# Transfers of 49 rows padded to 56 rows, a third buffer for stage D's constants, and longer planned landings

## The chip, the cores and the metric

The kernel runs on one core of one Trainium2 chip. The metric is the device time of one execution in microseconds (us). The core works with TensorE (PE: matrix products, its weight loads appear as PEld), VectorE (DVE), ScalarE (ACT), GpSimd (POOL), SyncE (SP, which here only issues transfers) and 16 DMA engines.

## What is computed

The reference chains two blocks on x of shape (8, 3136, 256), in float32:

```python
def _attn_ref(x, w_r, w_i, b_r, b_i):
    X = np.fft.rfft(x, axis=1)
    Yr = X.real @ w_r - X.imag @ w_i + b_r
    Yi = X.real @ w_i + X.imag @ w_r + b_i
    Y = shrink(Yr, 0.01) + 1j * shrink(Yi, 0.01)      # soft threshold
    return np.fft.irfft(Y, n=x.shape[1], axis=1)

def _moe_ref(x, U, V, w_ch1, w_ch2):
    xt = x.transpose(0, 2, 1)
    h = xt @ U @ V                                    # along the sequence, rank 32
    u = x + h.transpose(0, 2, 1)
    ch = np.maximum(u @ w_ch1, 0.0) @ w_ch2           # 256 -> 1024 -> 256
    return u + ch
```

(`shrink` stands for the reference's sign and maximum.)

## The kernel before, in words

The 3136 positions of one batch entry are split as 49 x 64, so that each Fourier transform becomes two steps of small matrix products. The work of one batch b goes through stages, and arrays in HBM lie between them:

- Stage A (`a_load` L702, `a_mm` L713): eight tiles `xt` (the first six of batch 1: `xa`) are loaded from x, each with two transfers of 49 rows of 4 KB, one into partitions 0 to 48 and one into 64 to 112. The 49-point transform with the matrix `fq` goes into PSUM (`psa`), is copied back over the tile, and four transfers of 49 rows of 2 KB put it into the HBM array `gd`. Batch 0 takes another way (`xx`, `t0t`).
- Stages B and C (`load_t`, `b_unit` L899, `mix_unit`, `c_unit` L982): 12 or 13 rounds per batch. `t` is loaded from `gd` and `fb` from the constants, 64-point transform (`psb`), channel mix (`psq`, `pst`), soft threshold (`rl`, `ys`, `yh`, `yl`), transform back (`psc`, copied to `zs`), store into the HBM array `zd`. A round begins on ACT with copies of `psb` to `xsh` and to the single buffer `ts`.
- Stage D (`z_load` L1071, `dt_load` L1078, `d_unit` L1086): eight tiles `zt` are loaded from `zd`, again with two transfers of 49 rows of 4 KB each, and six pieces `dt` of D's constants (128 rows, held in the HBM array `dud`, two buffers). The products `psd` give 49 positions, copied by ACT to `xq`, and 32 columns for U, summed by DVE into `pa`.
- P (`p_spread` L1156, `p_unit` L1164): DVE adds the parts of `pa` into `pr`, PE transposes it (`psp`), ACT and DVE make `pt` of it, the input of the product with V.
- Windows: six of 512 positions x 256 channels per batch (and one last one for the rest, 49 in all). `u_prep` adds the V product (`psv`) and splits into high and low parts (`oa`, `ob`, `oc`, `od`), `l1_chunks` is the first product of the channel block (`psx`, `psy`, `psz`), with `s`, `v`, `rh`, `rl` on ACT and DVE behind it, `l2_chunks` the second (`pso`). `out_unit` (L1731) transposes the result on DVE into the single buffer `os` (two instructions) and stores it with four transfers to `out_dram`.

While the windows of batch b run, stages B, C and D of batch b+1 and stage A of batch b+2 are put between them. The tiles `xt` and `zt` share five buffers (tag `xz`).

No engine's order is written out by hand. The kernel records all its operations, and a planner (`_Program.order`, L259) lays them out: a list scheduler that gives each operation a cost and a delay until its result is there (`cost`, L193), grants buffers, and serves on each engine the operation with the earliest due time. It goes forwards and backwards in time 12 times, takes the due times of the best pass, and issues everything in the order of its planned starts (`trace`, all from L537, so every row of the profile has that line, and groups are told apart by tiles). For a transfer the plan takes 64,000 elements per us and a landing 2.2 us behind that (L202, L504), and it lets a transfer start at most 16 us before it is due. SP issues all transfers but three, in one order, and each engine works its own list strictly in order.

Of the kernel before, what the change touches and what calls it, by code (L numbers as in the profile page):

```python
# [13 lines left out]
F32 = mybir.dt.float32  # L14
# [10 lines left out]
NB = 8  # L25
N1, N2 = 49, 64
NP = 98
NI = 32
D = 256
R = 32  # L30
# [10 lines left out]

STEPS_W = 8
K1 = 49
C81 = K1 + R

UNITS_D = [(0, 6), (6, 6), (12, 4), (16, 6), (22, 6), (28, 4)]
# [117 lines left out]
class _Program:  # L164
# [28 lines left out]
    def cost(self, op, out, ins):  # L193
        n = out.ids.size // out.shape[0] if isinstance(out, _View) else 1
        sb = not any(v.buf.space == "psum" for v in ins)
        op.move, op.port, op.fill, op.mode = 0.0, False, 0, 0
        if op.name == "dma_start":

            some = out if isinstance(out, _View) else ins[0]
            op.move = some.ids.size / 64000  # L200
            op.cost = 0.35 if op.eng == "act" else 0.6
            op.lag = 2.2 + op.move  # L202
        elif op.eng == "pe":
            if "tile_position" in op.kw:

                op.cost = (0.001668 * n + 0.005) / (4 if op.kw["lhsT"].shape[0] <= 64 else 2)
                op.mode = 2
            elif op.name == "matmul" and op.kw["lhsT"].dtype == F32:
                op.cost = 2 * max(0.111, 0.00084 * n)
                op.mode = 1  # L210
            else:
                op.cost = max(0.1118, 0.000422 * n)
            op.lag = 0.25
        elif op.eng == "act":
            op.cost = 0.062 + 0.000844 * n + (0.036 if sb else 0) + (0.098 if "bias" in op.kw else 0)
            op.lag = 0.2
        elif op.eng == "dve":

            op.port = sb and op.name != "transpose"
            slow = op.name == "transpose" and not sb  # L220
            op.cost = 0.07 + (0.00053 if op.name == "tensor_scalar" else 0.00158 if slow else 0.00104) * n
            op.lag = 0.185
        elif op.eng == "pool":
            op.port = op.name == "tensor_tensor"
            op.cost = 0.1 + (0.00223 if op.port else 0.0007) * n
            op.lag = 0.19
# [160 lines left out]
    def forward(self, units, size, tags, gap, late):  # L387

        engines = ("pe", "act", "dve", "pool", "sp")
        free = dict.fromkeys(engines, 0.0)  # L390
# [51 lines left out]
        while done < len(units):  # L442
            best = None
            for e in engines:
                now = max(free[e], moved - 2.0, landed[-8]) if e == "sp" else free[e]
                while future[e] and future[e][0][0] <= now:
                    _, l, k = _heapq.heappop(future[e])
                    _heapq.heappush(ready[e][units[k][0].mode if e == "pe" else units[k][0].port], (l, k))

                may = []  # L450
                if e == "pe":
                    for m in range(3):
                        if m == 2 and mode == 2 and not ready[e][2]:

                            soon = [f for f in future[e] if units[f[2]][0].mode == 2 and f[0] < now + TILED_WAIT]
                            if soon:
                                t, l, k = min(soon)
                                may = [(t, l, k, 4)]
                        elif ready[e][m]:
                            l, k = ready[e][m][0]  # L460
                            if m == 1 and mode == 1:
                                l -= STICK
                            elif m == 2:
                                l += -TILED_STAY if mode == 2 else TILED_IN
                            may.append((now, l, k, m))
                else:
                    if ready[e][0]:
                        may.append((now, *ready[e][0][0], 0))
                    if ready[e][1]:
                        may.append((max(now, port), *ready[e][1][0], 1))  # L470
                if not may and future[e]:
                    t, l, k = future[e][0]
                    may.append((max(t, port) if units[k][0].port else t, l, k, 3))
                if may and (best is None or min(may)[:2] < best[:2]):
                    best = *min(may), e
            if best is None:
                break
            t, l, k, kind, e = best
            if kind == 4:
                future[e].remove(next(f for f in future[e] if f[2] == k))  # L480
                _heapq.heapify(future[e])
            else:
                _heapq.heappop(future[e] if kind == 3 else ready[e][kind])
            u = units[k][0]
            if e == "pe":
                if t > free[e]:
                    self.idle.append((free[e], t - free[e], u))

                b = u.out.buf
                gap_, each = t - max(free[e], b.granted) - 0.2, 0.222  # L490
                if done_pe == 0:

                    gap_, each = gap_ - 0.6, 0.47
                done_pe += 1
                fill[k] = max(0, int(gap_ / each)) if b.first[0] is u and t < FILL else 0
            free[e] = t + sum(op.cost for op in units[k])
            if e == "pe":
                free[e] += SWITCH[mode][u.mode]
                mode = u.mode
            elif u.port:  # L500
                port = free[e]
            if u.move:
                moved = max(moved, t) + u.move
                u.lag = moved + 2.2 - free[e]  # L504
                landed.append(moved + 2.2)
            starts[k] = t
            done += 1
            for op in units[k]:
                op.start = t + op.at
                for s in op.succs:  # L510
                    if s.unit != k:
                        release(s.unit, t + gap(op, s) - s.at)
                bs = {}
                for v in list(op.args) + list(op.kw.values()):
                    if isinstance(v, _View) and v.buf.space != "dram":
                        bs[id(v.buf)] = v.buf
                for b in bs.values():
                    b.left -= 1
                    b.end = max(b.end, op.start + op.cost + op.lag)
                    if b.left == 0:  # L520
                        _heapq.heappush(slots[b.key], (b.end, k, b.slot, b))
                        grant(b.key)
# [18 lines left out]
def fft_mix_moe_kernel(  # L541
# [116 lines left out]
    bias = const.tile([128, 2, D], F32, name="bias")  # L658
    lam = const.tile([128, 1], F32, name="lam")

    gd = [dram.tile([N1, N2, D], F32, name=f"gd{k}") for k in range(2)]
    zd = [dram.tile([N1, N2, D], F32, name=f"zd{k}") for k in range(2)]
    dud = dram.tile([128, NI * C81], F32, name="dud")
    vd = dram.tile([2, R, 96 * NI], F32, name="vd")
    rd = dram.tile([128, 2, NB, 64], F32, name="rd")
# [31 lines left out]
            h, d = divmod(16 * k, 128)  # L697
            dve.transpose(out=t0[h][:, :, d : d + 16].rearrange("p k d -> p d k"), in_=ps.rearrange("p i d -> p d i"))

    xj = x.rearrange("b (n j i) d -> b j n i d", j=2, i=NI)  # L700

    def a_load(b, c):  # L702
        if b == 1 and c < 6:
            if c % 3 == 0:
                ahead_x[c // 3] = qp.tile([128, 12, D], F32, tag="xq", name=f"xa_{c}", bufs=3)
            xt = ahead_x[c // 3][:, 4 * (c % 3) : 4 * (c % 3) + 4]
        else:
            xt = fp.tile([128, 4, D], F32, tag="xz", name=f"xt_{b}_{c}", bufs=5)
        loads = [dma.dma_start(xt[64 * j : 64 * j + K1], xj[b, j, :, 4 * c : 4 * c + 4]) for j in range(2)]
        a_state[b, c] = xt  # L710
        return loads

    def a_mm(b, c, loads=()):  # L713
# [19 lines left out]
        for j in range(2):  # L733
            o = xt[:, 2 * j : 2 * j + 2]
            p = ps[j].rearrange("p (i d) -> p i d", i=2)
            if j:
                dve.tensor_copy(o, p)
            else:
                acopy(o, p)
            for e in range(2):  # L740
                i = 4 * c + 2 * e
                dma.dma_start(gv[j, :, i : i + 2], o[64 * e : 64 * e + K1])

    def a_half(b, half, loads):
        for c in range(4):
# [325 lines left out]
    def z_load(b, c):  # L1071
# [1 line left out]
        zt = fp.tile([128, 4, D], F32, tag="xz", name=f"zt_{b}_{c}", bufs=5)  # L1073
        zv = zd[b % 2].rearrange("k (j c i) d -> c j k i d", j=2, i=4)
        s_state[b, "z", c] = zt
        return [dma.dma_start(zt[64 * j : 64 * j + K1], zv[c, j]) for j in range(2)]

    def dt_load(b, t):  # L1078
        n0, n = UNITS_D[t]
        dt_ = mp.tile([128, 6 * C81], F32, tag="dt", name=f"dt_{b}_{t}", bufs=2)  # L1080
        dma.dma_start(dt_[:, 0 : n * C81], dud[:, n0 * C81 : (n0 + n) * C81])
        s_state[b, "d", t] = dt_

# [1 line left out]

    def d_unit(b, t, du, loads=()):  # L1086
        if t == 0:
            p_state[b] = qp.tile([128, 2, 3, R], F32, tag="pa", name=f"pa_{b}", bufs=2)
        n0, n = UNITS_D[t]
        hf = n0 // NH  # L1090
        if n0 % NH == 0:
# [62 lines left out]
        return us  # L1154

    def p_spread(b):  # L1156
        pr = qp.tile([128, 2, 4, R], F32, tag="pr", name=f"pr_{b}", bufs=1)
        pa = p_state[b]
        dve.tensor_tensor(out=pa[:, :, 0], in0=pa[:, :, 0], in1=pa[:, :, 1], op=ALU.add)
        a, c = [pa[:, :, k].unsqueeze(2).broadcast_to([128, 2, 4, R]) for k in (0, 2)]  # L1160
# [618 lines left out]
    for st in u0:  # L1779
        st()  # L1780
    setup_w()
    side = []

    def spread(units, lo, hi):
# [151 lines left out]
```

## Time and profile before

| What | us |
|---|---|
| Time before, median of 3 runs | 1676.95 |
| lowest and highest of them | 1668.06, 1677.43 |
| the profiled execution | 1668.87 |
| its span, first to last instruction | 1667.1 |

The profile is of one execution, 8.1 us below the median; 1.8 us of it lie outside the span. PE is busy in 96% of the span, DVE in 78%, ACT in 56%. A busy PE is not a PE at its peak: the ends of matmuls are modelled, and at the lower of TensorE's two clock levels (1.2 instead of 2.4 GHz) the same work takes twice as long and is counted as busy all the same. The column PEclk is the granted clock as a share of the full one. The share of the DMA engines is a mean over all 16.

### The profile page before, as it was taken

The page shows a single profiled execution, that of the slowest core. Times are in us where ns is not written, and L with a number is a line of the kernel's source. Part 1 is how long each engine was busy: PE and PEld are TensorE (multiplying, and loading weights), DVE is VectorE, ACT ScalarE, POOL GpSimd, SP SyncE. Part 2 cuts the span into 40 slices and gives each one's busy share as a digit, 9 for nine tenths or more (in the row PEclk, how much of TensorE's full clock was granted, in tenths as well). Part 3 has the DMA queues.
Part 4 walks back from the last instruction along what each step waited for, and adds up shares of the span by engine and source line. Part 5 has one row for each costly group of instructions (what it writes and reads, how often), then busy time and mean ns, then how long its engine had stood idle before and what let it go on. Part 6 is the DMA issues. An engine that isn't in the chain of part 4 may idle for free.

```text
span 1667.1 us, 37824 instructions
## 1 busy us (share of the span) xinstructions
PE 1607.3 (96%) x14546; PEld 1441.1 (86%) x14546; DVE 1299.8 (78%) x2478; ACT 932.2 (56%) x1982; POOL 449.6 (27%) x406
## 2 busy tenths in 40 slices
PE   8998999999989999899999999999999999999998
PEld 6967898899878889799888988989977999989997
DVE  7576888588956899678975889769985699957775
ACT  4764566556545665456654566555654566545453
POOL 1310333133311333123321133313331133412221
PEclk9989999999999999999998999999998999999999
DMA  9754343515552354522745244532555224530232
GB/s 232 218 178 159 93 145 96 159 44 131 164 152 83 118 162 116 151 59 66 175 147 156 79 143 128 145 89 68 148 146 166 66 67 98 111 113 13 53 75 47
DMA packets 229775, 198.30 MB, mean 119 GB/s; under 512 B 129594, under 2 KB 197728, under 8 KB 229596
## 3 DMA queue, kind: packets, MB, share of 16 engines
q1 hardware_dynamic: 226958, 195.02, 42.9%
q8 instruction: 115, 1.88, 0.5%
q10 hardware_dynamic: 2638, 0.86, 0.3%
q14 instruction: 64, 0.52, 0.1%
HBM read 118.92 MB, written 76.90 MB: 117 GB/s over the span
## 4 chain that ended last, share of the span: by engine, by line
PE 68%; DMA 14%; DVE 12%; issue 2%; ACT 2%; SPq 2%; DVEq 0%; ACTq 0%
PE pso L537 23%; PE psy L537 14%; PE psx L537 6%; PE psq L537 5%; DMA out_dram<-os 4%; PE psb L537 4%; PE psd L537 3%; DMA zt<-zd 3%; PE psa L537 3%; PE psz L537 3%; PE psc L537 3%; PE pst L537 3%; DVE ys L537 2%; SPq L537 2%; DVE rl L537 1%
## 5 line engine op out<-in xcount | busy, mean ns | idle before, releaser
L537 PE MATMUL pso<-rh,w2t 128*128 128x512 f32 x1568 | 410.2, 384 | 0.0
L537 PEld LDWEIGHTS pso<-rh,w2t 128*128 128x128 f32 x1568 | 276.8, 192 | 26.4
L537 PE MATMUL pso<-rl,w2t 128*128 128x512 f32 x784 | 235.0, 381 | 0.2 <-DVE rl L537 0.2
L537 POOL TENSOR_TENSOR yl<-ys,yh 128x512 fp32r<-128x512 f32 (+1 forms) x95 | 130.2, 1370 | 253.1 <-ACT yh L537 225.2
L537 DVE SCALAR_TENSOR_TENSOR ys<-tb,rl 64x256 f32<-64x256 f32 x350 | 180.5, 516 | 17.4 <-ACT rl L537 12.7
L537 ACT ACTIVATE rh<-s 128x512 fp32r<-128x512 f32 x196 | 122.1, 629 | 102.5 <-DVE s L537 97.1
L537 POOL TENSOR_TENSOR tl<-ts,th 128x256 fp32r<-128x256 f32 x88 | 71.1, 808 | 364.0 <-ACT th L537 298.7
L537 PEld LDWEIGHTS pso<-rl,w2t 128*128 128x128 f32 x784 | 149.3, 190 | 22.1 <-DVE rl L537 0.6
L537 DVE SCALAR_TENSOR_TENSOR rl<-s,rh 128x512 fp32r<-128x512 f32 x196 | 156.1, 802 | 13.6 <-ACT rh L537 11.4
L537 PE MATMUL psy<-odh,w1t 128*128 128x256 f32 x784 | 126.2, 284 | 7.7 <-DVE v L537 4.6
L537 PEld LDWEIGHTS psy<-odh,w1t 128*128 128x128 f32 x784 | 112.6, 194 | 22.1 <-DVE v L537 6.0
L537 PE MATMUL psq<-wmt,xsh 128*128 128x256 f32 (+1 forms) x704 | 123.2, 276 | 0.0
L537 PEld LDWEIGHTS psq<-wmt,xsh 128*128 128x128 f32 (+1 forms) x704 | 109.3, 191 | 1.7
L537 POOL TENSOR_TENSOR obl<-xq,obh 128x512 fp32r<-128x512 f32 x47 | 61.4, 1307 | 168.9 <-ACT obh L537 167.0
L537 ACT ACTIVATE xq<-psd 128x294 f32<-128x294 f32 (+1 forms) x192 | 69.7, 431 | 57.0 <-PE psd L537 55.1
L537 ACT ACTIVATE rh<-v 128x512 fp32r<-128x512 f32 x98 | 61.6, 629 | 68.6 <-DVE v L537 66.3
L537 DVE STREAM_TRANSPOSE os<-xq 128x512 f32<-128x512 f32 x96 | 65.2, 695 | 41.8 <-DMA out_dram<-os 24.9
L537 DVE TENSOR_TENSOR v<-v,psy 128x512 f32<-128x512 f32 x98 | 66.8, 681 | 39.2 <-PE psy L537 21.1
L537 PE MATMUL psq<-wmt,xsl 128*128 128x256 f32 (+1 forms) x352 | 96.8, 275 | 0.0
L537 POOL TENSOR_TENSOR odl<-tt,odh 128x512 fp32r<-128x512 f32 x48 | 63.9, 1331 | 119.2 <-ACT odh L537 117.8
L537 ACT ACTIVATE yh<-ys 128x512 fp32r<-128x512 f32 (+1 forms) x95 | 59.4, 625 | 63.7 <-DVE ys L537 60.2
L537 PE MATMUL psb<-fb,t 128*128 128x128 f32 (+1 forms) x700 | 93.0, 276 | 1.8 <-DMA t<-gd 1.8
(217 smaller groups left out, 3974.9 us busy)
## 6 DMA issues: line engine op xcount, KB each, us to landing
zt<-zd SPq DMA_DIRECT2D x128, 196.0 KB
zd<-zs SPq DMA_DIRECT2D x192, 128.0 KB
out_dram<-os SPq DMA_DIRECT2D x190, 128.0 KB
t<-gd SPq DMA_DIRECT2D x168, 128.0 KB
xt<-in_x_dram SPq DMA_DIRECT2D x100, 196.0 KB
gd<-xt SPq DMA_DIRECT2D x200, 98.0 KB
fb<-in_fb_dram SPq DMA_DIRECT2D x96, 128.0 KB
vw<-vd SPq DMA_DIRECT2D x96, 128.0 KB
```

The source lines that it names most:

```text
L537: call(*[real(a) for a in op.args], **{k: real(a) for k, a in op.kw.items()})
```

## The change

49 rows become 56 (`KP`) in the HBM arrays `gd` and `zd`, in the loads of `xt`, `xa` and `zt`, and in the stores to `gd`. The seven rows more hold what follows in x, zeros or the fill; no product reads them. The last batch of x has no rows behind it, and `zd` has no seven rows more until two new transfers fill them (from x, recorded behind `setup_w`), so batch 7 of stage A and batch 0 of stage D are loaded as 48 rows each and one short transfer of 2 rows for the 49th. `dt` gets a third buffer; for its room `pa` has one buffer instead of two and `pr` moves into the buffer of `ts`. The plan has 2.6 us instead of 2.2 for a landing.

```diff
+KP = 56
...
-            op.lag = 2.2 + op.move
+            op.lag = 2.6 + op.move
...
-                u.lag = moved + 2.2 - free[e]
-                landed.append(moved + 2.2)
+                u.lag = moved + 2.6 - free[e]
+                landed.append(moved + 2.6)
...
-    gd = [dram.tile([N1, N2, D], F32, name=f"gd{k}") for k in range(2)]
-    zd = [dram.tile([N1, N2, D], F32, name=f"zd{k}") for k in range(2)]
+    gd = [dram.tile([KP, N2, D], F32, name=f"gd{k}") for k in range(2)]
+    zd = [dram.tile([KP, N2, D], F32, name=f"zd{k}") for k in range(2)]
...
-    xj = x.rearrange("b (n j i) d -> b j n i d", j=2, i=NI)
+    xj = x.rearrange("b (n j i) d -> j (b n) i d", j=2, i=NI)
...
-        loads = [dma.dma_start(xt[64 * j : 64 * j + K1], xj[b, j, :, 4 * c : 4 * c + 4]) for j in range(2)]
+        nk = KP if b < NB - 1 else K1 - 1
+        n0, i = K1 * b, slice(4 * c, 4 * c + 4)
+        loads = [dma.dma_start(xt[64 * j : 64 * j + nk], xj[j, n0 : n0 + nk, i]) for j in range(2)]
+        if nk < K1:
+            loads.append(
+                dma.dma_start(xt.rearrange("(j n) i d -> n j i d", j=2)[nk], xj[:, n0 + nk, i])
+            )
...
-                dma.dma_start(gv[j, :, i : i + 2], o[64 * e : 64 * e + K1])
+                dma.dma_start(gv[j, :, i : i + 2], o[64 * e : 64 * e + KP])
...
-        return [dma.dma_start(zt[64 * j : 64 * j + K1], zv[c, j]) for j in range(2)]
+        nk = KP if b else K1 - 1
+        loads = [dma.dma_start(zt[64 * j : 64 * j + nk], zv[c, j, 0:nk]) for j in range(2)]
+        if nk < K1:
+            loads.append(dma.dma_start(zt.rearrange("(j n) i d -> n j i d", j=2)[nk], zv[c, :, nk]))
+        return loads
...
-        dt_ = mp.tile([128, 6 * C81], F32, tag="dt", name=f"dt_{b}_{t}", bufs=2)
+        dt_ = mp.tile([128, 6 * C81], F32, tag="dt", name=f"dt_{b}_{t}", bufs=3)
...
-            p_state[b] = qp.tile([128, 2, 3, R], F32, tag="pa", name=f"pa_{b}", bufs=2)
+            p_state[b] = qp.tile([128, 2, 3, R], F32, tag="pa", name=f"pa_{b}", bufs=1)
...
-        pr = qp.tile([128, 2, 4, R], F32, tag="pr", name=f"pr_{b}", bufs=1)
+        pr = fp.tile([128, 2, 4, R], F32, tag="ts", name=f"pr_{b}", bufs=1)
...
     setup_w()
+    for z in zd:
+        dma.dma_start(z[K1:KP], x[0, 0 : (KP - K1) * N2].rearrange("(k n) d -> k n d", k=KP - K1))
```

The planner lays everything out anew. Three places show it. The first is SP in stage D of batch 2, where loads of `zt`, stores to `gd` and the stores of one window's result (`os_6`) stand in one queue; before:

```order
L537 DMA zt_2_2_6298<-zd0_449 49x1024 x2
L537 DMA dt_2_1_6311<-dud_1052 128x486
L537 DMA zt_2_3_6321<-zd0_449 49x1024 x2
L537 DMA out_0_dram<-os_6_5857 32x16x64 x3
L537 DMA gd1_1126<-xt_3_7_5953 49x512 x4
L537 DMA out_0_dram<-os_6_5857 32x16x64
L537 DMA vw_11_6413<-vd_757 64x512 x2
L537 DMA dt_2_2_6453<-dud_1052 128x324
```

and with the change:

```order
L538 DMA zt_2_2_6302<-zd0_488 56x1024 x2
L538 DMA gd1_1148<-xt_3_7_5971 56x512 x3
L538 DMA zt_2_3_6329<-zd0_488 56x1024 x2
L538 DMA gd1_1148<-xt_3_7_5971 56x512
L538 DMA dt_2_1_6373<-dud_1078 128x486
L538 DMA out_0_dram<-os_6_5854 32x16x64 x4
L538 DMA dt_2_2_6412<-dud_1078 128x324
L538 DMA vw_11_6423<-vd_751 64x512 x2
```

The same transfers are there. The stores to `gd` have moved ahead of the window's stores, and the four stores of `os_6` now stand together.

The second is DVE a little later in the same stage, where the next window's transposes (`os_7`) have to wait until the stores of `os_6` have landed, the buffer being the same; before:

```order
L537 STREAM_TRANSPOSE os_7_6483<-xq_1_0_3883 128x16x32
L537 TENSOR_TENSOR s1_10_0_6341<-psz_10_0_6470,s1_10_0_6341 128x512
L537 TENSOR_TENSOR pa_2_6424<-pa_2_6424,psd_2_1_0_0_6438 128x96
L537 TENSOR_TENSOR pa_2_6424<-pa_2_6424,psd_2_1_0_1_6442 128x96
L537 TENSOR_TENSOR s5_10_0_6334<-psy_10_0_6324,s5_10_0_6334 128x512
```

and with the change:

```order
L538 TENSOR_TENSOR s1_10_0_6428<-psz_10_0_6437,s1_10_0_6428 128x512
L538 TENSOR_TENSOR v12_10_0_6419<-v12_10_0_6419,psy_10_0_6415 128x512
L538 STREAM_TRANSPOSE os_7_6459<-xq_1_0_3903 128x16x32 x2
L538 SCALAR_TENSOR_TENSOR rl_10_0_0_6473<-v12_10_0_6419,rh_10_0_0_6455 128x2x256
L538 SCALAR_TENSOR_TENSOR rl_10_0_0_6473<-s1_10_0_6428,rh_10_0_0_6455 128x2x256
```

The transposes have moved behind the sums `s1` and `v12`, and now two `rl` of the first channel product stand behind them.

The third is ACT at the seam between batches, where P of batch 2 (`pt_2`) meets the first round of stage B of batch 3 (`ts_3_0`); before:

```order
L537 ACTIVATE v12_11_1_7038<-psx_11_1_6948 128x512
L537 ACTIVATE xsh_3_0_7047<-psb_3_0_7034 128x256
L537 ACTIVATE ts_3_0_7051<-psb_3_0_7034 128x128 x2
L537 ACTIVATE xsh_3_0_7047<-psb_3_0_7034 128x256
L537 ACTIVATE s1_11_1_7062<-psy_11_1_7043 128x512
L537 ACTIVATE pt_2_7070<-psp_2_7055 128x256
```

and with the change:

```order
L538 ACTIVATE s5_11_1_7045<-psx_11_1_7029 128x512
L538 ACTIVATE pt_2_7051<-psp_2_7040 128x256
L538 ACTIVATE xsh_3_0_7058<-psb_3_0_7043 128x256
L538 ACTIVATE ts_3_0_7062<-psb_3_0_7043 128x128 x2
L538 ACTIVATE xsh_3_0_7058<-psb_3_0_7043 128x256
```

The copies to `ts` have moved behind P, whose `pr` lies in the same buffer now.

## Rows read from the trace of the kernel before

**Rows 1.** The page's head and busy time of the engines.

```profile
span 1667.1 us, 37824 instructions
...
PE 1607.3 (96%) x14546; PEld 1441.1 (86%) x14546; DVE 1299.8 (78%) x2478; ACT 932.2 (56%) x1982; POOL 449.6 (27%) x406
```

**Rows 2.** Busy time by stretch: the ten stretches in which PE waits.

```profile
core 0: us, PE busy (x) PEld busy (x) DVE busy (x) ACT busy (x) POOL busy (x), PEclk, DMA share, GB/s
110.00:150.00 40.00, 32.99 (x677) 30.25 (x675) 25.64 (x63) 16.13 (x39) 0.00 (x0) 0.96 0.52 182
300.00:330.00 30.00, 28.17 (x570) 25.03 (x569) 17.52 (x42) 17.41 (x38) 4.57 (x4) 1.00 0.64 192
430.00:450.00 20.00, 18.72 (x115) 13.43 (x115) 19.57 (x35) 10.95 (x23) 6.46 (x5) 0.91 0.53 142
475.00:510.00 35.00, 30.70 (x371) 27.60 (x370) 19.81 (x39) 14.05 (x29) 5.57 (x5) 0.90 0.60 172
660.00:710.00 50.00, 44.70 (x494) 39.49 (x493) 33.87 (x67) 22.68 (x44) 8.06 (x7) 0.97 0.56 151
820.00:835.00 15.00, 13.34 (x97) 10.29 (x95) 14.04 (x30) 8.77 (x20) 4.66 (x4) 1.00 0.64 148
870.00:900.00 30.00, 27.17 (x338) 24.50 (x337) 15.50 (x33) 12.46 (x27) 4.82 (x4) 0.83 0.64 191
1080.00:1100.00 20.00, 17.77 (x207) 16.26 (x206) 13.64 (x29) 8.03 (x18) 1.28 (x2) 0.83 0.50 138
1225.00:1300.00 75.00, 68.88 (x609) 59.65 (x608) 47.29 (x87) 33.81 (x68) 17.24 (x15) 0.91 0.52 153
1455.00:1500.00 45.00, 41.28 (x678) 36.77 (x678) 27.10 (x56) 22.02 (x47) 7.26 (x6) 1.00 0.37 112
sum 360.00, PE 323.73 PEld 283.26 DVE 233.99 ACT 166.31 POOL 59.91; mean PE 32.37 PEld 28.33 DVE 23.40 ACT 16.63 POOL 5.99
```

**Rows 3.** Busy time of eight other stretches, 150 to 1650 us, their sum.

```profile
sum 1120.00, PE 1112.60 PEld 1020.41 DVE 940.23 ACT 664.87 POOL 345.81; mean PE 139.07 PEld 127.55 DVE 117.53 ACT 83.11 POOL 43.23
```

**Rows 4.** Chain that ended last, 470 to 515 us: start us, us, what.

```profile
479.99 6.74 DMA zt<-zd
...
486.75 7.84 DMA out_dram<-os
...
494.65 2.30 DMA dt<-dud
...
498.28 1.65 PE psx L537 x6
```

**Rows 5.** Timeline of DVE, 484 to 500 us; in brackets idle time before.

```profile
496.94 0.71 DVE L537 STREAM_TRANSPOSE os<-xq 128x512 f32<-128x512 f32 x1 [5.18 <-DMA dt<-dud]
```

**Rows 6.** Chain that ended last, whole span, longest pieces.

```profile
111.67 7.92 DMA zt<-zd
...
1064.42 2.42 DMA zd<-zs
1067.88 5.76 DMA zt<-zd
...
1075.68 6.17 DMA out_dram<-os
...
1228.90 5.44 DMA gd<-xt
1234.74 6.42 DMA xt<-in_x_dram
```

**Rows 7.** Busy time by stretch: 1 KB and 4 KB rows mixed; `zt` loads alone.

```profile
58.00:63.00 5.00, 5.00 (x41) 4.81 (x40) 2.02 (x3) 4.59 (x10) 2.55 (x2) 1.00 0.94 260
...
1459.00:1463.00 4.00, 4.00 (x26) 3.66 (x25) 2.46 (x5) 1.66 (x3) 0.00 (x0) 1.00 0.44 179
```

**Rows 8.** The tile `gd`: its issues on SP, ns min/median/max.

```profile
L537 SPq DMA_DIRECT2D gd<-xt x200: 261/316/2207, 131.8 to 1274.4; - x100
```

**Rows 9.** Waits of PE: total us, times, longest.

```profile
PE psd L537 <- DMA zt<-zd: 5.2, 7, 1.4
```

## The prediction

> **What bounds the kernel now.** I read the page's head first: PE is busy 1607.3 of 1667.1 us [rows 1], so PE is the bound and idle 59.8 us, and no change that leaves the products alone can win more than that and what a slow clock costs. Next, busy time by stretch, to see where the idle time lies. Eight stretches of together 1120 us have PE busy 1112.6 us [rows 3]: 7.4 us lost. Ten others, 360 us in all, have 323.73 us busy [rows 2]: 36.3 us lost. They are the ends of stage A and the stages D, one group per batch, and seven of them show a granted clock (PEclk) under 1: 0.83 from 870 to 900 us means that a third of that stretch ran at 1.2 instead of 2.4 GHz. With c the granted clock and L the length, the work lost to it is (1-c) x L: 1.6, 1.8, 3.5, 1.5, 5.1, 3.4 and 6.8 us in the stretches from 110, 430, 475, 660, 870, 1080 and 1225 us, 23.7 in all. So the ten stretches lose 60 us to idling and clock together, less perhaps 4 that are counted twice where PE idles at the low clock.
>
> Then the chain that ended last, for what PE waits for there. From 480 us it runs through a load of `zt` (6.74 us), the store of a window's result (7.84), a piece of `dt` (2.30), and comes out on PE at 498.28 [rows 4]. The link is DVE: its next instruction is the transpose into the single buffer `os`, it sat idle 5.18 us before it [rows 5], and the sums that PE's next products need stood behind it in DVE's list. The same pair shows at 1067.88 and 1075.68 (`zt` 5.76, store 6.17), and `gd` 5.44 with `xt` 6.42 at 1228.90 [rows 6]. In batch 0 PE waits for `zt` itself, 5.2 us [rows 9], with a landing of 7.92 [rows 6].
>
> Is that much landing a fixed delay or a queue? A quiet store of `zd` lands in 2.42 us [rows 6], and `dt`, with 128 x 486 x 4 B = 243 KB larger than a load of `zt` (49 x 1024 x 4 B = 196 KB), in 2.30 [rows 4]. So more than half of what `zt` takes is queueing. From 1459 to 1463 us, with loads of `zt` alone in flight, the DMA share is 0.44 at 179 GB/s, while 0.94 at 260 GB/s were reached earlier with 128-row transfers in the mix [rows 7]. 0.44 x 16 is 7: a 49-row transfer uses seven of the sixteen engines, seven rows each, at 25.6 GB/s per engine, and everything queued behind it ends on the slowest seven.
>
> **The change, part by part.**
>
> **56 rows.** The row shows 49 rows shared out evenly, seven times seven; the widest even share of 56 rows over at most sixteen engines is four rows on each of fourteen, and I take that. The Trainium skill (DMA: Bandwidth & Descriptors, "Why a DMA increments its semaphore by 16 and not by 1") says that the engines are the largest number up to 16 that divides the outermost sizes of both sides; by it 49 gives 7, 56 gives 14, 48 gives 16, and the 0.44 agrees for 49. One load then occupies its engines 229 KB / (14 x 25.6 GB/s) = 0.64 us instead of 201 KB / 179 GB/s = 1.12 us, 43% less. Bounds: 0.88 us at the mixed stretch's 260 GB/s, 1.28 us if only seven engines take it. I take 0.64, since the row from 1459 us has the same 4 KB rows and the other has smaller ones in it.
>
> What that takes off the chains, queueing being what lies above 2.3 us: from 480 us (4.4 + 5.5) x 0.43 = 4.3 us, against 4.3 us of PE idle in that stretch; from 1068 us (3.5 + 3.9) x 0.43 = 3.2, against 2.2 idle; from 1229 us (3.1 + 4.1) x 0.43 = 3.1, against 6.1 idle, of which a second part near 1280 us is no such chain; in batch 0, with 48 rows on sixteen engines, 57% of 5.6 us for each of several `zt`, against 7.0 idle. At 0.88 us per load all these halve. Where the idling goes I let the clock loss go too, since the low clock appears only in stretches with idling.
>
> Two stretches I leave as they are: from 430 and 820 us DVE is busy 19.57 of 20 and 14.04 of 15 us [rows 2]; there DVE bounds, and a faster transfer wins nothing. Of the one from 1225 us (6.1 + 6.8) I take half. The others lose 7.0 + 1.6, 1.8, 4.3 + 3.5, 5.3 + 1.5, 2.8 + 5.1, 2.2 + 3.4 and 3.7 us (from 110, 300, 475, 660, 870, 1080, 1455 us); with 6.4 for the half that is 48.6, less the 4 counted twice: 45 us can be had, from eight stretches, 5.6 each.
>
> **What the new plan gives back.** The planner moves everything on every engine. In the DVE list the transposes of `os_7` now have two `rl` of the first product behind them; if the stores of `os_6` are late again, those and PE's second product wait. In the SP list the loads of `zt` and the stores to `gd` still stand right ahead of the window's stores. So I expect such stalls in some places still: three of eight at the mean 5.6 us, 17 us. That leaves 28.
>
> **The planned landing, 2.6 instead of 2.2 us,** costs nothing by itself on the chip; it lets consumers stand 0.4 us later. Its worth lies between nothing and 0.4 us for each transfer on a stalled chain, two each in ten stretches, 8 us. I count it within the 28.
>
> **A third `dt`.** It lets these loads go out a unit earlier. `dt` landed in 2.30 us and was last on one chain only [rows 4]: nothing, at best that piece.
>
> **`pr` in the buffer of `ts`, one `pa`.** The first copies to `ts` of the next batch must now wait for P, as ACT's list shows, where they stood before it. Behind them on ACT are the `rh` and `v` that the windows need. Bounds per seam: 0 (the plan knows of it and puts other work first) to 5.6 us (a stall of the kind from 1080 us: 2.2 idle + 3.4 clock). I take 0.4 us, near the low end, since by the plan P now precedes the copies and PE has products of two windows to go on with; 7 seams, 3 us.
>
> **More transfers.** Two to fill `zd` and sixteen short ones, 0.3 us of SP each by the issues of `gd` [rows 8]: 5 us of a SP that only issues. 224 stores to `gd` with 14 KB more, 112 loads of `zt` and 96 of `xt` or `xa` with 28 KB more, some 9 MB with the fills on 198 MB: it lies beside PE in stretches where the DMA share is 0.37 to 0.64. Nothing; if that cover were gone, 9 MB at 179 GB/s are 50 us spread over the span.
>
> **Sum.** 1668.9 - 28 + 3 = 1644 us on the scale of the profiled execution. That is 8 us under the median of the three runs, so the new median may also lie above what a quiet execution gives; I add a quarter of this, 2 us: 1646.
>
> **The rivals.**
>
> *Nearly all stalls go.* The 45 us come off and no new ones appear: 1624. For it: the chains save as much as PE idles in most stretches. Against: a new plan never fits the chip everywhere; the old one kept ten places.
>
> *The delay holds the chain, not the engines.* If landing were mostly a constant, more engines would leave it, and only the longer planned landing would help, 8 us, and the seams take 3 of them: 1664. For it: `zd` at 2.42 us shows that a constant of over two us is in every landing. Against: 196 KB took 5.8 to 7.9 us where 243 KB took 2.3. The Trainium skill (DMA: Bandwidth & Descriptors, "Anatomy of one DMA — SWDGE (gpsimd) path") gives 2.0 us plus the bytes at 436 GB/s, measured on another issue path; by it a load of `zt` would take an estimated 2.5 us with 49 rows and with 56, and the change would do nothing. The rows on `dt` agree with it, those on `zt` don't.
>
> *The seam becomes a stall.* Place: the first `ts` of each batch behind P. If P ends late, ACT stands at that copy, and each of seven seams costs the 5.6 us of the upper bound: 39 us, against 28 saved: 1668.9 - 28 + 39 = 1680. It decides from 4 us per seam; at 8 the time is over 1690. For it: the old list had `ts` ahead of `pt`. Against: the planner knows the buffer.
>
> *56 rows stay on seven engines.* Each queue grows by a seventh; on chains with some 10 us of queueing that is 1.4 us in each of eight stretches, 11 us: 1680. For it: the trace has no 56-row transfer. Against: 49 rows being spread as seven times seven.
>
> **How the numbers follow.** The forecast's own case, 1634 to 1660 us (the upper end is half the saving, as with 0.88 us per load: 1668.9 - 14 + 3 = 1658): 0.45. Nearly all stalls gone: 0.18. Delay, not engines: 0.20. The seam: 0.11. Seven engines: 0.06. A measurement of this kernel can tell about 1% from no change, so the bounds are 1660 and 1694 around the median of 1677. Faster: 0.45 + 0.18 and a fifth of the delay case, 0.67. Slower: half of the seam and half of the seven engines, 0.08. Same: 0.25. The range of 8 in 10 runs from the case with all stalls gone, 1622, into the delay case and the start of the two last, 1676.
>
> **What would show it.** Right: in a stretch with loads of `zt` alone the DMA share is near 0.88 and their landing on the chain 3 to 4 us; PE's idle time falls from 59.8 to some 40 us or less; fewer stretches with PEclk under 0.95; DVE's wait at `os` for stores falls. Wrong: a share of 0.44 again (seven engines); landings still 5 us and more (delay); idle time of ACT before `ts` with `psp` as what ended it (the seam); as much PE idle as before, in other places, with shorter landings (the plan gives it all back).

## The result, and the profile after

The changed kernel takes 1624.59 us (median of 4 runs, 1622.46 to 1626.98), the kernel before 1672.51 in runs beside it: a ratio of 0.971, 95% interval 0.967 to 0.975. It is faster by 2.9%. The forecast was 1646 us, faster, with 1622 to 1676 as the range.

The page's head and the engines' busy time, after:

```profile
span 1625.2 us, 37977 instructions
...
PE 1591.4 (98%) x14586; PEld 1430.2 (88%) x14586; DVE 1290.4 (79%) x2478; ACT 936.5 (58%) x1982; POOL 445.1 (27%) x406
```

Against [rows 1] the span is 41.9 us shorter. PE's idle time went from 59.8 to 33.8 us, 26.0 less, and its busy time fell by 15.9 us although it has 40 matmuls more. Work that was taken out can't be the reason; the clock is. The mean granted clock, before and after:

```profile
core 0: 1667.1 us, clock 0.981
...
core 0: 1625.2 us, clock 0.994
```

With c for it, (1 - c) times the span fell from 31.7 to 9.8 us.

Busy time by stretch, after, in ten stretches of the same stages as those of [rows 2] (ends of stage A and the stages D of all batches; the columns are the same). Most are longer than there and hold more work, 6326 matmuls in all against 4156, so the smaller loss doesn't come from work left out:

```profile
105.00:145.00 40.00, 35.80 (x713) 33.94 (x712) 25.11 (x62) 16.82 (x42) 0.00 (x0) 0.96 0.73 188
290.00:325.00 35.00, 34.25 (x654) 29.81 (x654) 22.79 (x51) 19.16 (x43) 4.76 (x4) 1.00 0.74 188
424.00:440.00 16.00, 16.00 (x118) 12.41 (x117) 13.72 (x26) 10.15 (x21) 5.96 (x5) 1.00 0.81 223
465.00:510.00 45.00, 44.84 (x727) 40.24 (x726) 29.78 (x64) 23.87 (x51) 8.95 (x8) 1.00 0.63 165
655.00:705.00 50.00, 49.13 (x750) 43.86 (x750) 33.35 (x70) 27.15 (x58) 9.67 (x8) 1.00 0.52 131
805.00:820.00 15.00, 15.00 (x117) 11.86 (x110) 14.80 (x31) 10.15 (x21) 5.40 (x5) 1.00 0.71 195
845.00:895.00 50.00, 50.00 (x757) 44.97 (x756) 31.73 (x70) 27.13 (x57) 9.21 (x8) 1.00 0.38 103
1045.00:1095.00 50.00, 48.55 (x752) 43.85 (x751) 31.10 (x67) 24.84 (x53) 4.96 (x5) 1.00 0.46 116
1186.00:1281.00 95.00, 93.47 (x1034) 78.27 (x1034) 66.79 (x129) 50.44 (x103) 20.20 (x17) 0.96 0.56 147
1420.00:1460.00 40.00, 40.00 (x704) 36.13 (x703) 24.41 (x58) 22.34 (x49) 6.11 (x5) 1.00 0.44 111
sum 436.00, PE 427.04 PEld 375.33 DVE 293.58 ACT 232.05 POOL 75.21; mean PE 42.70 PEld 37.53 DVE 29.36 ACT 23.20 POOL 7.52
```

They lose 436.00 - 427.04 = 9.0 us to idling, and 0.04 x 40 + 0.04 x 95 = 5.4 us to the clock: 14 us where the ten of before lost 60. That is the whole difference of the spans and a little more. Eight of the ten stretches stand at a granted clock of 1.00.

Whether the transfers take fourteen engines shows where only rows of 4 KB are in flight: loads of `xt` in the first two of these stretches, of `zt` in the third. After, busy time by stretch, the DMA share before last, GB/s last:

```profile
225.00:228.00 3.00, 3.00 (x27) 2.97 (x26) 2.96 (x6) 1.95 (x4) 1.60 (x2) 1.00 0.85 221
909.00:912.00 3.00, 3.00 (x24) 2.84 (x23) 0.15 (x1) 1.31 (x3) 1.28 (x1) 1.00 0.90 277
1048.00:1051.00 3.00, 3.00 (x64) 2.73 (x63) 1.56 (x4) 1.41 (x4) 0.00 (x0) 1.00 0.91 214
```

0.85 of 16 engines are 13.6, against 0.44, seven, in [rows 7]. But twice the engines moved far from twice the bytes: 214 to 277 GB/s against 179. At 214 GB/s a load of 229 KB takes 1.07 us, where 201 KB at 179 GB/s took 1.12.

The link to PE was DVE, waiting at the transpose into `os` for transfers to land. Waits of DVE in the kernel before (total us, times, longest us):

```profile
DVE os L537 <- DMA out_dram<-os: 24.9, 12, 6.9
...
DVE os L537 <- DMA vw<-vd: 10.2, 2, 5.1
...
DVE os L537 <- DMA dt<-dud: 5.2, 1, 5.2
DVE os L537 <- DMA t<-gd: 1.3, 1, 1.3
```

and after:

```profile
DVE os L538 <- DMA out_dram<-os: 7.1, 6, 2.5
```

41.6 us have become 7.1. (By the program these transposes wait for no transfer but the stores of the window before; the names `vw`, `dt` and `t` are the profile's inference.) One such pair is left on the chain of the whole span, in stage D of batch 5 (chain that ended last, after; start us, us, what):

```profile
1041.81 4.17 DMA zt<-zd
...
1046.00 7.84 DMA out_dram<-os
...
1053.96 1.30 DVE os L538 x2
...
1056.07 0.36 PE psd L538 x4
```

It is the pair of [rows 4] again, with `zt` at 4.17 instead of 6.74 us and the store at 7.84 us as before: seven loads of `zt` were still in flight ahead of that store, and by the trace they landed 1.07 us apart. Its price is within the 1.45 us that PE idles in the stretch from 1045 us.

### The profile page after: what moved, and what is told of

The parts are those of the page before. It is cut to its first block, busy times and chain, and to the rows that moved or that the text cites. A ratio compares the mean times of both kernels' runs of the same rounds, so it can differ in the third digit from the quotient of the medians.

```text
span 1625.2 us, 37977 instructions
## 1 busy us (share of the span) xinstructions
PE 1591.4 (98%) x14586; PEld 1430.2 (88%) x14586; DVE 1290.4 (79%) x2478; ACT 936.5 (58%) x1982; POOL 445.1 (27%) x406
## 4 chain that ended last, share of the span: by engine, by line
PE 39%; DVE 8%; issue 2%; DMA 1%; ACT 1%; SPq 0%; DVEq 0%; ACTq 0%
PE pso L538 15%; PE psy L538 8%; PE psx L538 4%; PE psd L538 2%; DVE ys L538 2%; PE psq L538 2%; PE psz L538 2%; PE psb L538 1%; PE psa L538 1%; DVE rl L538 1%; DVE tb L538 1%; PE pst L538 1%; PE psc L538 1%; DMA out_dram<-os 1%; DVE xq L538 1%
## 5 line engine op out<-in xcount | busy, mean ns | idle before, releaser
L538 POOL TENSOR_TENSOR yl<-ys,yh 128x512 fp32r<-128x512 f32 (+1 forms) x95 | 126.3, 1330 | 244.6 <-ACT yh L538 225.8
L538 DVE SCALAR_TENSOR_TENSOR ys<-tb,rl 64x256 f32<-64x256 f32 x350 | 176.7, 505 | 15.5 <-ACT rl L538 11.0
L538 PEld LDWEIGHTS pso<-rl,w2t 128*128 128x128 f32 x784 | 148.3, 189 | 21.9 <-DVE rl L538 0.8
L538 DVE SCALAR_TENSOR_TENSOR rl<-s,rh 128x512 fp32r<-128x512 f32 x196 | 146.7, 751 | 19.9 <-ACT rh L538 18.1
L538 PEld LDWEIGHTS psy<-odh,w1t 128*128 128x128 f32 x784 | 111.2, 192 | 15.1 <-issue 6.5
L538 DVE SCALAR_TENSOR_TENSOR rl<-v,rh 128x512 fp32r<-128x512 f32 x98 | 83.0, 847 | 15.5 <-ACT rh L538 13.8
```

Source lines behind the costliest of these rows:

```text
L538: call(*[real(a) for a in op.args], **{k: real(a) for k, a in op.kw.items()})
```

## The experiments

Two theories stood against each other. *Engines*: a transfer spread over fourteen engines ends sooner, and the stalls go with the queue. *Plan*: the planner laid everything out anew, with longer landings and another buffer, and the new order is what avoids the stalls. They could be told apart because the plan and the transfers can be set separately. In e1 and e2 a transfer is planned in one form and issued in another, and every engine's list is the same, instruction for instruction, as in the kernel whose plan it has, but for the two fills of `zd` that e2 adds on SP. A second question came up with e4: whether all parts of the change help. The runs were made in three groups, each on another chip, and the kernel before took 1671.09, 1662.20 and 1672.24 us in them (medians), so times are compared within a group, or with the ratio beside them.

**e1: the plan of after, 49 rows issued.**

```diff
-        loads = [dma.dma_start(zt[64 * j : 64 * j + nk], zv[c, j, 0:nk]) for j in range(2)]
+        mk = min(nk, K1)
+        loads = [
+            dma.dma_start(
+                zt[64 * j : 64 * j + nk],
+                zv[c, j, 0:nk],
+                wide=(zt[64 * j : 64 * j + mk], zv[c, j, 0:mk]),
+            )
+            for j in range(2)
+        ]
...
-            call(*[real(a) for a in op.args], ...)
+            call(*[real(a) for a in (op.wide or op.args)], ...)
```

(The plan works with the first form, the chip gets the one named `wide`; `mk` is the smaller of `nk` and 49. The same for `xt`, `xa` and the stores to `gd`.)

> The changed kernel's plan, instruction for instruction in the same order on every engine, but the transfers of gd, xt, xa and zt that have 56 rows in it move 49 rows (the 48 and 2 rows of batch 0's zt and batch 7's xt stay, the fills stay). Theory 'engines' (the gain comes from fourteen engines in place of seven): most of the gain is lost, 1650 to 1680 us, landings of zt on SP's queue over 5 us again and DVE's wait at os over 25 us. Rival 'plan' (the gain comes from the new order and its longer landings): 1624 to 1632 us.

Measured: 1641.55 us (1638.23 to 1644.47), ratio 0.982 (0.976 to 0.987). The share where `zt` is alone is that of seven engines again, PE's busy time is up to 1601.0 us, and so is DVE's wait at `os`. Busy time by stretch, e1:

```profile
673.00:676.00 3.00, 3.00 (x24) 2.84 (x23) 1.03 (x2) 1.23 (x2) 1.05 (x1) 1.00 0.45 154
```

Its waits of DVE:

```profile
DVE os L539 <- DMA out_dram<-os: 17.6, 11, 3.1
...
DVE os L539 <- DMA zt<-zd: 2.9, 1, 2.9
```

With the same lists on all engines, seven engines instead of fourteen cost 17 us against the 1624.59 of the changed kernel (ratio 0.982 against 0.971). But e1 is also 29.5 us under the kernel before in its group. So neither theory has it all: with seven engines the new plan alone takes away a good half of the loss. Its 20.5 us at `os` lie between the 41.6 of before and the 7.1 of after. (Batch 0's `zt` keeps its 48 rows in e1, so its stretch is in those 29.5 us.)

**e2: the plan of before, 56 rows issued.**

```diff
+                zt[64 * j : 64 * j + K1],
+                zv[c, j, 0:K1],
+                wide=(zt[64 * j : 64 * j + KP], zv[c, j]) if b else None,
...
+            if later and op.start > 170:
+                later = False
+                self.fill_zd(engines["sp"])
```

> The kernel before, its plan kept on every engine, but its 49-row transfers move 56 rows, except zt of batch 0 and xt of batch 7, which stay at 49; the two fills of zd are put into SP's list behind batch 1's first stages. Theory 'engines': 1630 to 1645 us, DVE's wait at os (40 us in all before) under 15 us. Rival 'plan': 1664 to 1677 us, the ten stretches idle as before.

Measured: 1627.24 us (1620.08 to 1630.05), ratio 0.973 (0.968 to 0.978), 43.9 us under the kernel before. That is a little below the range of *engines*. *Plan* alone falls: no instruction of before changed its place, and nearly the whole gain is there. The page's busy time of PE in e2, and the share from a stretch with `zt`:

```profile
PE 1585.4 (98%) x14546; PEld 1425.1 (88%) x14546; DVE 1300.7 (80%) x2478; ACT 931.8 (57%) x1982; POOL 450.7 (28%) x406
```

```profile
1039.00:1042.00 3.00, 3.00 (x18) 2.68 (x17) 3.00 (x5) 1.63 (x4) 2.46 (x2) 1.00 0.83 214
```

The number of matmuls is that of before, the span 1624.2 us: PE idles 38.8 us instead of 59.8 and is busy 21.9 us less, the granted clock being 0.996. DVE still waits 22.0 us at `os` there, more than the expected 15, but shorter each time (4.1 us at most, 6.9 before), and PE idles less.

What the 56 rows change in a transfer shows best here, the order being the same. In the trace a store to `gd` that was queued behind another landed 0.57 us after it before and 0.34 us after it in e2 (medians, from the last updates of their semaphores); a load of `zt` behind another 1.14 and 1.01 us. So the stores, with rows of 2 KB, end 41% sooner, the loads, with rows of 4 KB, 11%. No run has 56 rows in the stores alone or the loads alone, so which of them took the stalls away is not shown.

**e3: the planned landings of 2.6 us alone.**

```diff
-            op.lag = 2.2 + op.move
+            op.lag = 2.6 + op.move
...
-                u.lag = moved + 2.2 - free[e]
-                landed.append(moved + 2.2)
+                u.lag = moved + 2.6 - free[e]
+                landed.append(moved + 2.6)
```

> The kernel before with planned landings of 2.6 us instead of 2.2 and nothing else. Theory 'engines': 1655 to 1680 us, a new order with about as many stalls. Rival 'plan': 1625 to 1645 us.

Measured: 1654.41 us (1651.60 to 1658.38), ratio 0.991 (0.988 to 0.994): 16.7 us, more than expected of *engines* and less than of *plan*. DVE's waits at `os` in e3 are about as long as before:

```profile
DVE os L537 <- DMA out_dram<-os: 17.5, 9, 4.9
...
DVE os L537 <- DMA dt<-dud: 9.8, 1, 9.8
DVE os L537 <- DMA zt<-zd: 9.8, 2, 6.7
...
DVE os L537 <- DMA vw<-vd: 4.0, 1, 4.0
```

41.1 us in all, against 41.6. So PE loses less by waits of the same length; what in the order does so is not shown. e3 is also one plan set against one other, and plans differ by some us without any such reason (e7).

**e4: the 56 rows alone.**

```diff
-            op.lag = 2.6 + op.move
+            op.lag = 2.2 + op.move
...
-        dt_ = mp.tile([128, 6 * C81], F32, tag="dt", name=f"dt_{b}_{t}", bufs=3)
+        dt_ = mp.tile([128, 6 * C81], F32, tag="dt", name=f"dt_{b}_{t}", bufs=2)
...
-            p_state[b] = qp.tile([128, 2, 3, R], F32, tag="pa", name=f"pa_{b}", bufs=1)
+            p_state[b] = qp.tile([128, 2, 3, R], F32, tag="pa", name=f"pa_{b}", bufs=2)
...
-        pr = fp.tile([128, 2, 4, R], F32, tag="ts", name=f"pr_{b}", bufs=1)
+        pr = qp.tile([128, 2, 4, R], F32, tag="pr", name=f"pr_{b}", bufs=1)
```

(the changed kernel is the minus side; the two other uses of 2.6 go back as well)

> The changed kernel with planned landings of 2.2 us, two dt buffers, two pa buffers and pr in a buffer of its own: 56 rows alone. Theory 'engines': 1620 to 1640 us. Rival 'plan' (the 2.6 us or the third dt buffer carry it): 1655 to 1677 us.

Measured: 1610.28 us (1608.64 to 1612.48), ratio 0.964 (0.959 to 0.968). It is below what either theory gave, and below the whole change: the 2.6 us and the buffers seemed to cost some 14 us once the rows are 56. Eight further runs look into that.

**e5 and e6: one of the two undone in the changed kernel.** e5 has the first hunk of e4's diff, e6 the other three.

> The changed kernel with planned landings of 2.2 us again; 56 rows and the new buffers stay. If the 2.6 us are what makes the changed kernel slower than its 56 rows alone (1610 us in the run before, 1625 for the whole change): 1608 to 1614 us. If the buffers are it: 1620 to 1630. If it is the luck of a plan: anything from 1608 to 1635.

> The changed kernel with two dt buffers, two pa buffers and pr in a buffer of its own again; 56 rows and 2.6 us stay. If the buffers (ts waiting for P) are what costs: 1608 to 1614 us. If the 2.6 us are: 1620 to 1630. Luck of a plan: anything from 1608 to 1635.

Measured: e5 1623.07 us (ratio 0.976, 0.974 to 0.978), e6 1624.23 (0.977, 0.975 to 0.979). Neither came to 1610. By what was expected each points to the other, so no single part is the cost: either of them is enough for it, or the plan's luck is.

**e7 and e8: the plans shaken.** The kernel has a hook that adds random numbers to the due times.

```diff
-CHANGES = ()
+CHANGES = ((1, 0.1, 0.0, 1e9),)
```

> The changed kernel with random numbers of 0.1 us standard deviation added to the plan's due times before its last pass, by the hook the kernel has for that: another order, nothing else changed. If the 15 us between whole change and 56 rows alone come from the parts: within 4 us of 1625. If they are luck of a plan: more than 6 us off, either way.

> 56 rows alone (planned landings 2.2 us, old buffers) with the same random numbers on the due times. If the parts decide: within 4 us of 1610. If luck of a plan: more than 6 us off, most likely above, since 1610 was then a good draw.

Measured: the whole change shaken 1616.78 us (ratio 0.972, 0.971 to 0.974), 56 rows alone shaken 1610.75 (0.969, 0.967 to 0.971). A small stir of the due times moved the whole change by about 8 us, by which luck of a plan can be that large; 56 rows alone stayed where it was.

**e9 to e12: both kernels again on one chip, and each with a second draw** (`CHANGES = ((2, 0.1, 0.0, 1e9),)`).

> The changed kernel as it is, on the same chip as the next three, since the kernel before took 1671 us in one group of runs and 1662 in the other. If the whole change is really behind its 56 rows alone: at least 6 us over e10. If the difference was the chip's: within 4 us of e10.

> 56 rows alone (planned landings 2.2 us, old buffers), as in e4, beside e9. If 2.6 us and buffers together cost: 6 to 15 us under e9. If not: within 4 us of it.

> 56 rows alone with another draw of the 0.1 us random numbers on the due times. If the parts decide: within 4 us of e10, and under all three plans of the whole change. If luck of a plan: more than 6 us off.

> The whole change with the same draw. If the parts decide: within 4 us of e9 and over all three plans of 56 rows alone. If luck of a plan: its distance to e9 is as large as that between e9 and e10.

Measured, in this group:

| | 56 rows alone | whole change |
|---|---|---|
| as it is | e10: 1612.30 us, 0.962 (0.959 to 0.966) | e9: 1623.36 us, 0.970 (0.967 to 0.973) |
| second draw | e11: 1614.98 us, 0.965 (0.962 to 0.967) | e12: 1622.02 us, 0.969 (0.966 to 0.973) |

The 11 us between e10 and e9 are not the chip's. Over three plans of each, 56 rows alone took 1611.3 (mean of e4 and e10), 1610.75 and 1614.98, the whole change 1624.0 (mean of its first runs and e9), 1616.78 and 1622.02: 1612.3 and 1620.9 in the mean, 8.6 us apart, and every plan of the one below every plan of the other. Within a kind they differ by up to 4.2 and 7.2 us, and the nearest pair (1614.98 and 1616.78) was not run side by side. So it is likely that the 2.6 us and the buffers together cost some 8 us here, not certain with three draws each, and which of the two is open.

Where the time goes is shown only in part. e10's page has PE busy 1580.8 us of a span of 1610.1. Of the 15.1 us between this span and that of after, 4.5 are idle time of PE (29.3 us against 33.8) and 10.6 busy time at the same number of matmuls. The granted clock is 0.998, and (1 - c) times the span, 3.2 us against 9.8, accounts for some 6 of these.

In PE's waits one for DVE's `rl` stands out; after, in e10, and in e6, which has the longer landings and the old buffers:

```profile
PE psy L538 <- DVE rl L538: 7.6, 11, 1.1
...
PE psy L538 <- DVE rl L538: 2.9, 6, 0.9
...
PE psy L538 <- DVE rl L538: 3.3, 3, 2.3
```

All four runs of the whole change have 7.3 to 8.7 us of it, the four of 56 rows alone 2.2 to 4.8. But e6 has little of it as well and was no faster, so this wait is not the whole cost. Nor is DVE's wait at `os`; in e10:

```profile
DVE os L538 <- DMA out_dram<-os: 11.9, 9, 5.6
```

It is longer in each of the four runs of 56 rows alone (11.5 to 15.5 us in all) than in those of the whole change (4.5 to 7.8), and the whole change is the slower one. So that wait tells where the kernel before stalled, and not how two kernels with 56 rows compare. In these runs 56 rows alone is the fastest version.

## Why the prediction was right in its direction, and 21 us short

The measured 1624.59 us lies in the range, near its lower end of 1622, but not in the forecast's own case (1634 to 1660 us, chance 0.45). It lies where the rival with nearly all stalls gone was put (1624 us, 0.18).

- **What bounds, and where.** Right. The ten stretches had 60 us of loss, and 46 us of it went, in these stretches.
- **Seven engines become fourteen.** Right: 0.44 became 0.85, and 0.83 in e2. The rule of the Trainium skill (DMA: Bandwidth & Descriptors, "Why a DMA increments its semaphore by 16 and not by 1") holds for 49 and 56 rows here. The case with seven engines is out.
- **One load in 0.64 us instead of 1.12.** Wrong for the loads. The term took over the 25.6 GB/s of each of seven engines for each of fourteen. The measured 221 GB/s on 13.6 engines are 16 for each, and a load of `zt` queued behind another landed 1.04 us after it (median; 1.14 before). About the 43% came only for the stores to `gd`: 0.57 and 0.33 us. The sign "landing 3 to 4 us" did not come either: from issue to the last update of its semaphore a load of `zt` took 4.9 us (median of batches 1 to 7), 5.8 before.
- **`dt` landing in 2.30 us.** Misread. The 2.30 us are a piece of the chain: by its semaphore this load, issued at 494.65 us, landed at 498.24. What ended DVE's wait at 496.94 us [rows 5] was the last store of the window before, issued at 492.53 and landed at 496.91. So `dt` does not show that a larger load lands in 2.3 us; `zd` at 2.42 us is left for that base.
- **45 us can be had.** Right in size: e2 changes the transfers and nothing of the order, leaves batch 0's loads of `zt` as they were, and gains 43.9 us. But the working doesn't carry that size. By it the gain halves already at 0.88 us per load, and a load took 1.04 in the median; that all of the 45 came is luck as far as the working goes, and the stores to `gd` may have their part in it. That the clock loss goes with the idling held: e2's clock is 0.996. e2 also rules out the case that only the longer planned landing helps.
- **What the new plan gives back, 17 us.** This is the term that failed. It was put as "three of eight at the mean 5.6 us". One such chain is left, worth at most 1.45 us of PE's idling and no clock. With the old plan nearly the same transfers gave 1627.24 us, with the new 1624.59: the new plan gave nothing back. It might be that a new order has little to run into once transfers land nearer to what the plan takes them to need; no run shows that. Without those 17 us, the seams and the allowance for the median, the sum is 1624, the time that the rival with nearly all stalls gone had.
- **The planned landing, at most 8 us.** Too small for the old transfers, if e3's 16.7 us are not in part the luck of its plan; DVE's waits for landings didn't shrink there. With 56 rows it gave nothing that the runs show: undone, the time stayed at 1623 (e5).
- **The seam, 3 us, up to 39.** The stall did not come. ACT's idle time before its copies to `ts` rose from 3.9 to 7.3 us, but what ended it was `psb`, `tl` and, for 0.5 us, `odl`, as this group of the lines shows, before and after; P is not among them:

```profile
L537 ACT ACTIVATE ts<-psb 128x128 f32<-128x128 f32 x174 | 39.5, 281 | 3.9 <-POOL tl L537 2.0 <-PE psb L537 1.9
...
L538 ACT ACTIVATE ts<-psb 128x128 f32<-128x128 f32 x174 | 39.8, 280 | 7.3 <-PE psb L538 3.9 <-POOL tl L538 2.9 <-POOL odl L538 0.5
```

  Whether the shared buffer has its part in the 8 us that the landings and buffers together may cost stays open.
- **Two stretches bounded by DVE.** Right for the transfers: a faster one wins nothing there. In e2, with the order of before, nearly the same DVE work as from 430 and 820 us has PE still idle for 1.5 us in each, against 1.3 and 1.7 before:

```profile
418.00:438.00 20.00, 18.48 (x125) 13.39 (x125) 19.52 (x34) 11.70 (x27) 7.01 (x6) 1.00 0.69 182
799.00:814.00 15.00, 13.53 (x101) 10.23 (x99) 13.86 (x27) 8.64 (x19) 4.67 (x4) 1.00 0.68 154
```

  After, in the new order, PE idles not at all there (16.00 of 16 and 15.00 of 15 us), though DVE is busy 14.80 us in the second. So the new order took away what the prediction left in place.

## What to carry to other kernels

Look at the DMA share in a stretch with one kind of transfer in flight before looking at its bytes: 0.44 meant seven of sixteen engines here, and padding the rows was worth more than the 10 MB it added. But don't take the rate of an engine among seven for that of an engine among fourteen: here it fell from 25.6 to between 15 and 19 GB/s with rows of 4 KB. When a change goes through a planner, issue the new transfers with the old plan and the old transfers with the new plan; here that showed a gain of 44 us by the transfers alone and one of 30 by the plan with its 48-row batch, and no more than 48 by both together, so they remove much the same stalls. And try each part of a change without the others: here the version without the longer landings and the new buffers is the fastest, likely by some 8 us.

## What was not expected

Transfers of 56 rows on fourteen engines cost more on the queue that issues. Issues on SP (ns min/median/max), before, in the kernel with 49 rows:

```profile
L537 SPq DMA_DIRECT2D zt<-zd x128: 262/302/2472, 109.6 to 1477.1; - x128
```

and after, with 56:

```profile
L538 SPq DMA_DIRECT2D zt<-zd x136: 302/386/1952, 101.9 to 1434.4; - x136
```

The stores to `gd` went from 316 to 385 ns [rows 8], and in e1, with after's plan and 49 rows, they took 311 (after, then e1):

```profile
L538 SPq DMA_DIRECT2D gd<-xt x200: 306/385/2326, 111.6 to 1237.8; - x100
...
L539 SPq DMA_DIRECT2D gd<-xt x200: 262/311/1369, 116.6 to 1254.5; - x100
```

So it is the transfer, not the order. With 432 such transfers and some 75 ns each, an estimate from these medians, that is about 32 us more of SP's time over the run, beside PE here.

A shake of 0.1 us on the due times went with 8 us less for the whole change, half a percent of the time. A single comparison of two planned orders says little below that.
